# Splits and block sums around the change from the expert layer to the GLU: all on VectorE, begun in the seventh expert; the GLU's out-product between the two parts of a step

## The chip, the cores and the metric

The kernel runs on one core of a Trainium2 chip. The metric is the device time of one execution in microseconds, the median of several runs. Engines are named as in the profile: PE (TensorE matmul) with PEld (its weight loads), DVE (VectorE), ACT (ScalarE), POOL (GpSimd) and SP (SyncE, which issues most DMAs).

## What is computed

Three layers follow each other: a gated linear attention, a mixture of 8 experts of which each token takes one, and a bilinear GLU with an output matrix. The change touches the last expert steps and the GLU.

```python
# experts: N = 3072 tokens, D = 384, F = 1024
h = np.maximum(x[mask] @ w1[e], 0.0)
out[mask] = gate_w[mask, None] * (h @ w2[e])
# GLU: w1, w2 (384 x 1024), w3 (1024 x 1024), w_out (1024 x 384)
a = x @ w1
b = x @ w2
h = a * b @ w3
return (h @ w_out).astype(np.float32)
```

The kernel multiplies w3 by w_out beforehand (the tile wp), so the GLU is (a * b) @ wp.

## The kernel before

Every matrix product is made of three passes (PASSES): each fp32 operand is split into a high half (ACT rounds it to fp32r, L142) and a lower half (the rest, a subtraction on DVE or POOL, L143); the passes are high x high, high x lower and lower x high. `split` does both, and its last argument names the engine of the lower half, POOL (G) by default.

Experts (L1094 on). For each of 8 experts, 8 steps s run over 128 hidden columns: `g1_step` (9 matmuls into hb; ACT writes the high half of h, L994; DVE the lower, L995), then `g2_step` of the step before (9 matmuls into acc, which read h). A phase is half an expert: its two weight matrices come by DMA into two tiles `stg` (pool `stage`, two buffers), are split into wh and wl, and the splits stand in a queue of generators, `wsplit`, of which each step pulls a few. `bg` is a second such queue: it turns and multiplies w3 into wp (`w3_turn`, `w3_times` on PE, with pieces on ACT, DVE and POOL). Phases 16 and 17 are the two halves of the GLU's weights, kept in scratch `gd` (`prefetch_g`): `plain_sets` splits the first matrix, `mixed_sets` makes sums and differences of blocks of both (S1 to S4, A22, A23), since the GLU forms a and b from seven block products in place of more. `x_sets` does the same for a pair of token blocks: from six blocks of the expert output xd it makes nine split tiles, x0 to x8 (B11, T3, T2, T1, B21, B31, T4, B22, B32). Tile names end in h for the high and l for the lower half.

GLU (L1215 on). Tokens go in 3 pairs (n) of 2 x 512. The first part of a pair has 8 groups s. A group has 12 products (pa, pb, pc, pd), then 21 that add to them; ACT copies pa, pb and pd, DVE and POOL form the sums, and DVE multiplies. The product of the first block is split at once into a pair of tiles (abh and abl, in turn with two halves of a `stg` tile) and goes through `out_step` (12 matmuls of 384 columns with wp, L1199) behind the products of the next group; the product of the second block is kept in `later`. The second part of a pair splits the eight `later` blocks (`to_pair`) and runs 8 more out_steps (o2), while `x_sets(n + 1)` prepares the next pair; `store` copies the results and writes them by an indirect DMA from POOL's queue. m1t, m5t, m7t and ut are slices of two tiles xT. Of PSUM's two groups of four banks one takes a pair's products and then o2, the other o1; from pair to pair they change places.

Each engine runs its instructions in the order in which the code issues them; a tile that is written again waits for its readers.

## Time and profile before

| | us |
|---|---|
| median of 3 runs (736.49 to 738.60) | 738.53 |
| the profiled execution | 738.52 |
| its span (first to last instruction) | 736.5 |
| PE busy | 705.5 (96%) |
| DVE busy | 455.4 (62%) |
| ACT busy | 359.8 (49%) |
| POOL busy | 399.8 (54%) |

The page also cuts the span in 40 slices of 18.4 us; each digit is the busy share in tenths:

```profile
PE   8999999999999999999999787999999999999995
DVE  8989899976555555435424877455754448645551
ACT  5797878845657666546545542222422224322230
POOL 5366877784877677475456654222552223622243
PEclk9999999999999999999999998999999999999998
```

The experts run from about 177 to 429 us, the GLU from 429 to 728 us; the last 8 us hold the last stores.

### The profile page before, as it was taken

The numbers are of one execution on the slowest core, as the hardware profiler recorded it, in microseconds if no ns is written. First come the engines' busy times: TensorE is split into PE (matmuls) and PEld (weight loads), VectorE is DVE, ScalarE is ACT, GpSimd is POOL, SyncE is SP. The second block draws the span as 40 slices with busy tenths as digits, with TensorE's granted clock in tenths as the row PEclk, the third lists the DMA queues.
The fourth block names the chain that finished last, engine by engine and source line by source line (L and its number), as shares of the span: only waits on it lengthen the run. The fifth ranks groups of instructions, "written<-read, shape, count | busy, mean of one in ns | idle before, by whom it ended". The sixth has DMA issues, their size and how long they took to land.

```text
span 736.5 us, 13521 instructions
## 1 busy us (share of the span) xinstructions
PE 705.5 (96%) x5098; PEld 644.4 (87%) x5098; DVE 455.4 (62%) x828; ACT 359.8 (49%) x745; POOL 399.8 (54%) x464
## 2 busy tenths in 40 slices
PE   8999999999999999999999787999999999999995
PEld 7999988889999999999999665888888888888895
DVE  8989899976555555435424877455754448645551
ACT  5797878845657666546545542222422224322230
POOL 5366877784877677475456654222552223622243
PEclk9999999999999999999999998999999999999998
DMA  8999999653876776473442230000110001100001
GB/s 170 209 224 214 230 222 230 170 195 96 271 228 211 252 241 222 148 233 107 123 129 87 86 88 0 1 0 1 44 43 1 1 0 44 45 0 1 1 33 56
DMA packets 132032, 85.73 MB, mean 116 GB/s; under 512 B 106481, under 2 KB 114681, under 8 KB 131961
## 3 DMA queue, kind: packets, MB, share of 16 engines
q1 hardware_dynamic: 128489, 74.55, 37.3%
q0 software_dynamic: 3072, 9.46, 3.4%
q8 instruction: 42, 0.69, 0.4%
q10 hardware_dynamic: 400, 0.79, 0.3%
q14 instruction: 29, 0.24, 0.1%
HBM read 70.57 MB, written 14.22 MB: 115 GB/s over the span
## 4 chain that ended last, share of the span: by engine, by line
PE 58%; DVE 7%; DMA 3%; ACT 3%; issue 2%; POOL 2%; SPq 1%; POOLq 0%; DVEq 0%; ACTq 0%
PE acc L1006 11%; PE hb L992 10%; PE ob L1199 10%; PE pa L1161 7%; PE pb L1161 6%; PE pd L1161 6%; PE pc L1161 4%; DMA stg<-in_moe_w_dram 3%; PE wpb L185 3%; DVE wl L143 1%; PE xb L979 1%; ACT wh L142 1%; DVE stg L143 1%; DMA stg<-gd 1%; DVE h L1205 1%
## 5 line engine op out<-in xcount | busy, mean ns | idle before, releaser
L143 POOL TENSOR_TENSOR wl<-stg,wh 128x384 fp32r<-128x384 f32 (+1 forms) x110 | 128.5, 1197 | 56.4 <-ACT wh L142 54.6
L1164 POOL TENSOR_TENSOR xT<-xT,xT 128x512 f32<-128x512 f32 x48 | 62.8, 1308 | 132.9 <-ACT xT L1171 129.5
L1006 PE MATMUL acc<-h,wh 128*128 128x448 f32 (+7 forms) x384 | 105.5, 352 | 8.1 <-DVE h L995 7.9
L992 PE MATMUL hb<-xT,wh 128*128 128x448 f32 (+7 forms) x384 | 102.5, 348 | 0.0
L995 DVE SCALAR_TENSOR_TENSOR h<-hb,h 128x448 fp32r<-128x448 f32 (+7 forms) x64 | 37.0, 577 | 85.7 <-ACT h L994 85.4
L1006 PEld LDWEIGHTS acc<-h,wh 128*128 128x128 f32 x384 | 70.5, 188 | 12.8 <-DVE h L995 10.7
L142 ACT CAST wh<-stg 128x384 fp32r<-128x384 f32 (+1 forms) x121 | 61.1, 561 | 25.6 <-DMA stg<-in_moe_w_dram 21.0
L992 PEld LDWEIGHTS hb<-xT,wh 128*128 128x128 f32 x384 | 70.8, 188 | 1.4
L992 PE MATMUL hb<-xT,wl 128*128 128x448 f32 (+7 forms) x192 | 66.7, 348 | 0.0
L1006 PE MATMUL acc<-h,wl 128*128 128x448 f32 (+7 forms) x192 | 66.6, 347 | 0.0
L994 ACT ACTIVATE h<-hb 128x448 fp32r<-128x448 f32 (+7 forms) x64 | 32.3, 505 | 53.1 <-PE hb L992 52.9
L1164 DVE TENSOR_TENSOR xT<-xT,pc 128x512 f32<-128x512 f32 x48 | 32.8, 683 | 39.4 <-PE pc L1161 39.2
L1164 DVE TENSOR_TENSOR xT<-xT,pb 128x512 f32<-128x512 f32 x24 | 16.5, 689 | 64.3 <-PE pb L1161 64.2
L1199 PE MATMUL ob<-wp,abh 128*128 128x384 f32 x176 | 46.0, 343 | 0.0
L1199 PE MATMUL ob<-wp,stg 128*128 128x384 f32 x228 | 44.3, 338 | 1.1 <-DVE stg L143 1.1
L516 POOL TENSOR_SCALAR_AFFINE_SELECT am<-am 128x512 f32<-128x512 f32 x48 | 29.4, 637 | 25.7 <-ACT am L515 25.7
L1199 PEld LDWEIGHTS ob<-wp,stg 128*128 128x128 f32 x228 | 39.6, 188 | 3.8 <-DVE stg L143 3.0
L1170 ACT COPY xT<-pa 128x512 f32<-128x512 f32 x24 | 14.0, 585 | 56.2 <-PE pa L1161 53.8
L1206 POOL DMA_INDIRECT out_dram<-h,didx x24 | 24.2, 1010 | 27.0 <-DVE h L1205 24.6
L185 PE MATMUL wpb<-wo,w3t 128*128 128x384 f32 x192 | 36.8, 340 | 0.0
L1187 ACT CAST abh<-xT 128x512 fp32r<-128x512 f32 x13 | 8.1, 621 | 58.7 <-DVE xT L1164 40.6
L992 PEld LDWEIGHTS hb<-xT,wl 128*128 128x128 f32 x192 | 36.1, 188 | 0.7
(365 smaller groups left out, 1838.4 us busy)
## 6 DMA issues: line engine op xcount, KB each, us to landing
stg<-in_moe_w_dram SPq DMA_DIRECT2D x30, 768.0 KB
raw<-in_moe_w_dram SPq DMA_DIRECT2D x28, 512.0 KB
xs<-xsd SPq DMA_DIRECT2D x8, 675.5 KB
q<-in_q_dram SPq DMA_DIRECT2D x24, 192.0 KB
k<-in_k_dram SPq DMA_DIRECT2D x24, 192.0 KB
v<-in_v_dram SPq DMA_DIRECT2D x24, 192.0 KB
f<-in_f_logit_dram SPq DMA_DIRECT2D x23, 192.0 KB
raw<-in_moe_w_out_dram SPq DMA_DIRECT2D x8, 384.0 KB
```

The costliest lines, as they stand in the source:

```text
L142: A.copy(out=hi, in_=src)
L143: eng.tensor_tensor(out=lo, in0=src, in1=f32(hi), op=ALU.subtract)
L185: PE.matmul(out=o, lhsT=t[:, x, j, :], rhs=wo[:, y, j, :], start=(j + n == 0), stop=(j == KF - 1 and n == 2))
L516: G.affine_select(out=m[:, hb], in_=m[:, hb], pattern=[[0, NP], [1, P]], compare_op=ALU.is_ge, fill=0.0, base=0, channel_multiplier=-1)
L992: PE.matmul(out=b, lhsT=w[x][:, kk, cs], rhs=xT[e][y][:, kk, :], start=(kk + n == 0), stop=(kk == KD - 1 and n == 2))
L994: A.activation(out=h[0], in_=b, func=AF.Relu)
L995: V.scalar_tensor_tensor(out=h[1], in0=b, scalar=0.0, in1=f32(h[0]), op0=ALU.max, op1=ALU.subtract)
L1006: PE.matmul(out=acc[d], lhsT=w[x][:, s % 4, d * P:(d + 1) * P], rhs=hs[s][y], start=(s + n == 0), stop=(s == KF - 1 and n == 2))
L1161: PE.matmul(out=o, lhsT=w[a][i][:, cs], rhs=x[b][j], start=(first and m == 0), stop=(last and m == 2), skip_group_check=True)
L1164: eng.tensor_tensor(out=out, in0=a, in1=b, op=op)
L1199: PE.matmul(out=o[t], lhsT=ab[x][:, t * P:(t + 1) * P], rhs=wp[:, y, s, :], start=(s + m == 0), stop=(s == KF - 1 and m == 2), skip_group_ ...
L1206: ins = G.indirect_dma_start(out=out, out_offset=bass.IndirectOffsetOnAxis(ap=didx[:, j:j + 1], axis=0), in_=r, in_offset=None,)
```

## The change

- In `x_sets`, `plain_sets` and `mixed_sets` every lower half and every sum is DVE's; so are all lower halves of phases 13 to 15 (`ph > 2 * E - 4`; before, POOL's but for half of phase 15).
- `x_sets(0)` begins at step 3 of the seventh expert, with the pools of the GLU opened there, and a table X_AT spreads its 13 pieces over the seventh and eighth expert. Before, it took 3 pieces in each step of the eighth, some of them on POOL.
- `bg` is pulled 4 times per step in the sixth expert (before 3) and drained at step 3 of the seventh (before, step 0 of the eighth).
- The pulls of `wsplit` at the end change: in the eighth expert's steps 4 to 7 they are 3, 0, 3, 3 and 2 more at the end (before 4, 4, 4, 9), in the GLU's first groups 3, 3, 3, 9 (before 6, 9). The sums of `mixed_sets` come in another order and are made in the loaded tiles.
- In a GLU group, `out_step` of the group before stands between the 12 and the 21 products; the lower half of the product stands behind the last sum on DVE; one pair of tiles serves all first blocks.
- In the second part, the first out_step of o2 comes ahead of the last of o1, o1's results are copied by ACT, one per step, and POOL splits nothing.

```diff
-                split(t[:, i], h[:, i], l[:, i], V if ph in (0, 2 * E - 1) and i % 2 else G)
+                split(t[:, i], h[:, i], l[:, i], V if ph > 2 * E - 4 or ph == 0 and i % 2 else G)
...
     def plain_sets(hl, r):
         for kk in range(KD):
-            split(r[:, kk], hl[0][:, kk], hl[1][:, kk], V if kk % 2 else G)
+            split(r[:, kk], hl[0][:, kk], hl[1][:, kk], V)
             yield
...
+        if hf == 0:
+            s3(a, 2)
+            yield
+            one("A23", b, 2, (bh[:, 2], bl[:, 2]))
+            yield
+            s1()
+            s2()
+            yield
+            ch, cl = third[hf]()
+            one("S3", a, 2, (ch[:, 0], cl[:, 0]))
+            yield
+            one("S2", b, 0, (ch[:, 1], cl[:, 1]))
+            yield
+            one("S1", b, 2, (bh[:, 0], bl[:, 0]))
+            yield
+            one("A22", b, 1, (bh[:, 1], bl[:, 1]))
+            yield
+            s4(a, 1)
+            one("S4", a, 1, (ch[:, 2], cl[:, 2]))
+            yield
+            return
...
+        X_AT = (0, 0, 0, 1, 3, 0, 2, 0, 1, 0, 2, 2, 0, 3, 0, 0)
...
-            plus, e1, e2 = (V, G, V) if n else (G, V, V)
...
-                if e == E - 1:
-                    if s == 0:
-                        bg.drain()
-                        close_w3()
-                        cvx.close()
-                        open_m2()
-                        xs_ids(e)
-                        ahead_x = x_sets(0)
-                    step(ahead_x, 3)
+                if (e, s) == (E - 2, 3):
+                    bg.drain()
+                    close_w3()
+                    cvx.close()
+                    open_m2()
+                    ahead_x = x_sets(0)
+                if (e, s) == (E - 1, 2):
+                    xs_ids(e)
...
-                bg.pull(3)
-                wsplit.pull((4, 4, 4, 9)[s % 4] if e == E - 1 and s >= KF // 2 else (0 if e or s else 2, 3, 2, 2)[s % 4])
+                bg.pull(4 if e == E - 3 else 3)
+                wsplit.pull((3, 0, 3, 3)[s % 4] if e == E - 1 and s >= KF // 2 else (0 if e or s else 2, 3, 2, 2)[s % 4])
+                if e >= E - 2:
+                    step(ahead_x, X_AT[s + (e - E + 2) * KF])
...
+            if e == E - 1:
+                wsplit.pull(2)
             g2_step(e, KF - 1)
...
             tt(G, m7t, m7t, m5t)
+            then()
             product(ab, "A12", "B21", False, False)
...
-            then()
             tt(V, m1t, ut, bt)
             tt(V, m1t, m1t, ab, ALU.mult)
-            pair = next_pair()
-            A.copy(out=pair[0], in_=m1t)
+            A.copy(out=pairs[0][0], in_=m1t)
             tt(V, m5t, ut, at)
-            tt(V, pair[1], m1t, f32(pair[0]), ALU.subtract)
             tt(V, m7t, m7t, bb)
+            tt(V, pairs[0][1], m1t, f32(pairs[0][0]), ALU.subtract)
...
-                    wsplit.pull((6, 9, 0, 0, 0, 0, 0, 0)[s])
+                    wsplit.pull((3, 3, 3, 9, 0, 0, 0, 0)[s])
...
-            second = {0: to_pair(later[0], next_pair())}
-            out_step(o1, last, KF - 1)
+            out_step(o2, second[0], 0)
             if end:
                 for s in range(1, KF):
-                    second[s] = to_pair(later[s], free[s], G if s % 2 == 0 else V)
-                    if s == 2:
-                        store(o1, 2 * n * NT)
-                for s in range(KF // 2):
+                    second[s] = to_pair(later[s], free[s])
+                out_step(o1, pairs[0], KF - 1)
+                store(o1, 2 * n * NT, copy=A.copy)
+                for s in range(1, KF // 2):
                     out_step(o2, second[s], s)
...
             else:
                 ahead_x = x_sets(n + 1)
-                for s in range(KF):
+                second[1] = to_pair(later[1], pairs[1])
+                out_step(o1, pairs[0], KF - 1)
+                step(ahead_x, 1)
+                for s in range(1, KF):
                     if s + 1 < KF:
-                        second[s + 1] = to_pair(later[s + 1], next_pair())
+                        second[s + 1] = to_pair(later[s + 1], pairs[(s + 1) % 2 == 1])
                     out_step(o2, second[s], s)
-                    if s == 0:
-                        store(o1, 2 * n * NT)
+                    if s <= NT:
+                        store(o1, 2 * n * NT, (s - 1,), copy=A.copy)
                     step(ahead_x, 2)
```

How the instructions stand on two engines, before and after, at three places. A row is a line, an operation, its output, its inputs and its shape.

DVE in the middle of the eighth expert, before: h is the lower half that PE reads, x0l to x8l are `x_sets`, wl the weights' lower halves; the rest of them stand on POOL.

```order
L995 SCALAR_TENSOR_TENSOR h_5996<-hb,h_5995 128x376
L143 TENSOR_TENSOR x2l<-xd,x2h 128x512
L143 TENSOR_TENSOR x7l<-xd,x7h 128x512
L143 TENSOR_TENSOR x4l<-xd,x4h 128x512
L143 TENSOR_TENSOR wl<-stg,wh 128x384
L995 SCALAR_TENSOR_TENSOR h_6029<-hb,h_6028 128x376
L143 TENSOR_TENSOR x6l<-xd,x6h 128x512
L143 TENSOR_TENSOR x5l<-xd,x5h 128x512
L143 TENSOR_TENSOR wl<-stg,wh 128x384
L995 SCALAR_TENSOR_TENSOR h_6065<-hb,h_6064 128x376
```

The same engine and place, after:

```order
L1031 SCALAR_TENSOR_TENSOR h_5988<-hb,h_5987 128x376
L143 TENSOR_TENSOR wl<-stg,wh 128x384 x2
L143 TENSOR_TENSOR x7l<-xd,x7h 128x512
L143 TENSOR_TENSOR x4l<-xd,x4h 128x512
L1031 SCALAR_TENSOR_TENSOR h_6029<-hb,h_6028 128x376
L143 TENSOR_TENSOR wl<-stg,wh 128x384 x2
L1101 TENSOR_TENSOR xd<-xd 128x512
L143 TENSOR_TENSOR x6l<-xd,x6h 128x512
L1031 SCALAR_TENSOR_TENSOR h_6063<-hb,h_6062 128x376
L143 TENSOR_TENSOR wl<-stg,wh 128x512 x3
L1031 SCALAR_TENSOR_TENSOR h_6096<-hb,h_6095 128x376
```

Between two h stand up to four operations in both; all weights' halves and the subtraction (L1101, L1065 before) are now among them, and part of x_sets has gone to the seventh expert.

PE at the turn from one GLU group to the next, before: pc is the last product of a group, ob the out-product of that group's predecessor, pa the first product of the next.

```order
L1161 MATMUL pc<-x8h,wh 128x512
L1161 MATMUL pc<-x8l,wh 128x512
L1161 MATMUL pc<-x8h,wl 128x512
L1199 MATMUL ob<-wp,stg 128x384 x12
L1161 MATMUL pa<-x0h,wh 128x512
L1161 MATMUL pa<-x0l,wh 128x512
```

PE after, inside a group: pd ends the 12 products, pa<-x4h begins the 21.

```order
L1195 MATMUL pd<-x3h,wl 128x512
L1231 MATMUL ob<-wp,abh 128x384 x2
L1231 MATMUL ob<-wp,abl 128x384
L1231 MATMUL ob<-wp,abh 128x384 x2
L1231 MATMUL ob<-wp,abl 128x384
L1231 MATMUL ob<-wp,abh 128x384 x2
L1231 MATMUL ob<-wp,abl 128x384
L1231 MATMUL ob<-wp,abh 128x384 x2
L1231 MATMUL ob<-wp,abl 128x384
L1195 MATMUL pa<-x4h,wh 128x512
```

The 12 out matmuls have moved from the end of a group (of its predecessor's product) into the middle of the next.

DVE in one GLU group, before (xT_6214 holds m1t and m5t, xT_6215 holds m7t and ut):

```order
L1164 TENSOR_TENSOR xT_6215<-xT_6214,pc 128x512
L1164 TENSOR_TENSOR xT_6214<-xT_6215,pb 128x512
L1164 TENSOR_TENSOR xT_6214<-xT_6214,pa 128x512
L1164 TENSOR_TENSOR xT_6214<-xT_6215,pd 128x512
L1164 TENSOR_TENSOR abl<-xT_6214,abh 128x512
L1164 TENSOR_TENSOR xT_6215<-xT_6215,pc 128x512
L1164 TENSOR_TENSOR xd<-xT_6214,xT_6215 128x512
```

After:

```order
L1198 TENSOR_TENSOR xT_6215<-xT_6214,pc 128x512
L1198 TENSOR_TENSOR xT_6214<-xT_6215,pb 128x512
L1198 TENSOR_TENSOR xT_6214<-xT_6214,pa 128x512
L1198 TENSOR_TENSOR xT_6214<-xT_6215,pd 128x512
L1198 TENSOR_TENSOR xT_6215<-xT_6215,pc 128x512
L1198 TENSOR_TENSOR abl<-xT_6214,abh 128x512
L1198 TENSOR_TENSOR xd<-xT_6214,xT_6215 128x512
```

The lower half abl and the sum with pc have changed places.

## Rows read from the trace of the kernel before

**Rows 1.** Busy time by stage: stretch, its length, each engine's busy us, clock, DMA.

```profile
core 0: us, PE busy (x) PEld busy (x) DVE busy (x) ACT busy (x) POOL busy (x), PEclk, DMA share, GB/s
394.90:429.50 34.60, 26.87 (x146) 24.70 (x145) 26.86 (x32) 16.60 (x33) 18.75 (x14) 1.00 0.23 70
429.50:512.80 83.30, 77.83 (x338) 64.48 (x337) 46.37 (x65) 22.94 (x41) 28.95 (x21) 0.96 0.07 19
536.10:609.90 73.80, 73.80 (x337) 62.21 (x336) 36.35 (x56) 18.78 (x32) 24.39 (x24) 1.00 0.03 11
512.80:536.10 23.30, 22.24 (x122) 20.73 (x122) 18.11 (x29) 9.94 (x19) 11.21 (x13) 1.00 0.09 35
706.80:728.40 21.60, 21.55 (x122) 21.18 (x120) 9.12 (x17) 4.84 (x10) 11.86 (x18) 1.00 0.15 56
```

**Rows 2.** PE's waits from 395 us on: waiter, releaser, total us, times, longest.

```profile
PE acc L1006 <- DVE h L995: 7.7, 6, 2.1
PE pa L1161 <- ACT xT L1170: 3.2, 2, 2.8
PE pc L1161 <- DVE xT L1164: 2.2, 1, 2.2
```

**Rows 3.** Timeline of PE, eighth expert and first GLU pair: start, us, instruction, idle before.

```profile
399.11 0.51 PE L1006 MATMUL acc<-h,wh 128*128 128x376 f32 x2
...
399.63 0.51 PE L992 MATMUL hb<-xT,wh 128*128 128x376 f32 x2
...
447.29 0.78 PE L1161 MATMUL pc<-x8h,wh 128*128 128x512 f32 x1 [2.23 <-DVE xT L1164]
...
457.56 0.80 PE L1161 MATMUL pa<-x4h,wh 128*128 128x512 f32 x1 [2.82 <-ACT xT L1170]
```

**Rows 4.** The table by stretch, as rows 1, behind the two gaps.

```profile
448.00:452.00 4.00, 4.00 (x17) 3.76 (x16) 1.34 (x3) 0.23 (x1) 0.00 (x0) 0.66 0.00 0
456.00:460.00 4.00, 2.44 (x6) 1.98 (x7) 2.24 (x3) 2.08 (x4) 3.48 (x3) 0.70 0.00 0
```

**Rows 5.** Timelines of DVE, POOL and ACT in the eighth expert.

```profile
406.75 1.78 DVE L143 TENSOR_TENSOR x7l<-xd,x7h 128x512 fp32r<-128x512 f32 x1
...
410.33 0.53 DVE L995 SCALAR_TENSOR_TENSOR h<-hb,h 128x376 fp32r<-128x376 f32 x1
412.23 0.69 DVE L143 TENSOR_TENSOR x6l<-xd,x6h 128x512 fp32r<-128x512 f32 x1 [1.36 <-ACT x6h L142]
412.84 0.69 DVE L143 TENSOR_TENSOR x5l<-xd,x5h 128x512 fp32r<-128x512 f32 x1
...
404.53 4.86 POOL L143 TENSOR_TENSOR wl<-stg,wh 128x512 fp32r<-128x512 f32 x3
...
413.45 0.47 ACT L994 ACTIVATE h<-hb 128x376 fp32r<-128x376 f32 x1
```

**Rows 6.** Timelines of PE and POOL in one GLU group of the second pair.

```profile
592.60 0.39 PE L1161 MATMUL pa<-x0h,wh 128*128 128x512 f32 x1
...
595.39 0.39 PE L1161 MATMUL pa<-x4h,wh 128*128 128x512 f32 x1
...
600.22 2.25 PE L1199 MATMUL ob<-wp,stg 128*128 128x384 f32 x12
602.30 0.39 PE L1161 MATMUL pa<-x0h,wh 128*128 128x512 f32 x1
...
594.85 1.29 POOL L1164 TENSOR_TENSOR xT<-xT,xT 128x512 f32<-128x512 f32 x1 [6.97 <-ACT xT L1171]
```

**Rows 7.** The page's costliest groups: busy us, mean ns of one, idle before.

```profile
L1170 ACT COPY xT<-pa 128x512 f32<-128x512 f32 x24 | 14.0, 585 | 56.2 <-PE pa L1161 53.8
```

**Rows 8.** Timeline of DVE in the second part of the first pair.

```profile
532.80 1.37 DVE L143 TENSOR_TENSOR stg<-xT,stg 128x512 fp32r<-128x512 f32 x1 [0.35 <-ACT stg L142]
```

**Rows 9.** Timelines of PE and DVE in the sixth expert, transposes of w3 and their split.

```profile
346.46 1.04 PE L174 MATMUL w3b<-ident,g 128*128 128x128 f32 x8
347.26 0.60 PE L992 MATMUL hb<-xT,wh 128*128 128x388 f32 x2
...
347.72 1.29 DVE L177 TENSOR_TENSOR w3t<-w3b,w3t 128x512 fp32r<-128x512 f32 x2 [1.57 <-ACT w3t L176]
```

More of the change, by code (lines that the diff above doesn't have):

```diff
@@ L367, in mixed_sets, with one, s3, s1 @@
             d["A1%d" % (kk + 1)] = ah[:, kk], al[:, kk]
-        def one(n, t, kk, hl, eng):
+        def one(n, t, kk, hl):
             d[n] = hl
-            split(t[:, kk], hl[0], hl[1], eng)
-        one("A23", b, 2, (bh[:, 2], bl[:, 2]), V)
+            split(t[:, kk], hl[0], hl[1], V)
+        def s3(t, kk):
+            V.tensor_tensor(out=t[:, kk], in0=a[:, 0], in1=b[:, 0], op=ALU.subtract)
+        def s1():
+            V.tensor_tensor(out=b[:, 2], in0=b[:, 0], in1=b[:, 1], op=ALU.add)
@@ new lines, in s2, with s4 @@
+        def s2():
+            V.tensor_tensor(out=b[:, 0], in0=b[:, 2], in1=a[:, 0], op=ALU.subtract)
+        def s4(t, kk):
+            V.tensor_tensor(out=t[:, kk], in0=a[:, 1], in1=b[:, 0], op=ALU.subtract)
+        if hf == 0:
[19 more added lines that the diff above has]
+            return
@@ L374, in mixed_sets @@
+        one("A23", b, 2, (bh[:, 2], bl[:, 2]))
         yield
-        one("A22", b, 1, (bh[:, 1], bl[:, 1]), G)
+        one("A22", b, 1, (bh[:, 1], bl[:, 1]))
         yield
-        V.tensor_tensor(out=b[:, 2], in0=b[:, 0], in1=b[:, 1], op=ALU.add)
-        V.tensor_tensor(out=b[:, 1], in0=a[:, 0], in1=b[:, 0], op=ALU.subtract)
+        s1()
+        s3(b, 1)
         yield
-        V.tensor_tensor(out=b[:, 0], in0=b[:, 2], in1=a[:, 0], op=ALU.subtract)
+        s2()
+        one("S1", b, 2, (bh[:, 0], bl[:, 0]))
@@ L381, in mixed_sets @@
         yield
-        one("S1", b, 2, (bh[:, 0], bl[:, 0]), V)
+        s4(b, 2)
+        ch, cl = third[hf]()
+        one("S3", b, 1, (ch[:, 0], cl[:, 0]))
         yield
-        V.tensor_tensor(out=b[:, 2], in0=a[:, 1], in1=b[:, 0], op=ALU.subtract)
-        ch, cl = third[hf]()
+        one("S2", b, 0, (ch[:, 1], cl[:, 1]))
         yield
-        for i, (n, kk) in enumerate((("S3", 1), ("S2", 0), ("S4", 2))):
-            one(n, b, kk, (ch[:, i], cl[:, i]), V if i == 2 else G)
-            yield
+        one("S4", b, 2, (ch[:, 2], cl[:, 2]))
@@ L391, in prefetch @@
+        yield
     def prefetch(ph):
@@ L1193, in group @@
                 tt(V, t, m5t[:, c], m7t[:, c], ALU.mult)
-            return pair
         def out_step(o, ab, s, ts=range(NT)):
@@ L1199, in out_step, with store @@
                     PE.matmul(out=o[t], lhsT=ab[x][:, t * P:(t + 1) * P], rhs=wp[:, y, s, :], start=(s + m == 0), stop=(s == KF - 1 and m == 2), skip_group_check=True)
-        def store(o, j0, ts=range(NT)):
+        def store(o, j0, ts=range(NT), copy=V.tensor_copy):
             for t in ts:
@@ L1204, in store @@
                 r = f32(m1p.tile([P, CAP], F32R, name=f"h{j % 2}", bufs=3))[:, 0:DM]
-                V.tensor_copy(out=r, in_=o[t])
+                copy(out=r, in_=o[t])
                 ins = G.indirect_dma_start(
@@ L1217, in attn_moe_glu_kernel @@
             o1 = [bank2(1 - n % 2, DM, "ob") for _ in range(NT)]
-            last = None
             for s in range(KF):
-                pair = group(n, s, lambda: s and out_step(o1, last, s - 1))
+                if s == KF - 1:
+                    second = {0: to_pair(later[0], pairs[1])}
+                group(n, s, lambda: s and out_step(o1, pairs[0], s - 1))
                 if n == 0:
-                    wsplit.pull((6, 9, 0, 0, 0, 0, 0, 0)[s])
-                if n == 0 and s == 1:
+                    wsplit.pull((3, 3, 3, 9, 0, 0, 0, 0)[s])
+                if n == 0 and s == 3:
                     t = stage[0].tile([P, KD, 512], F32R, tag="stg", name="stg")
                     pairs.append([t[:, i] for i in range(2)])
-                last = pair
             o2 = [bank2(n % 2, DM, "ob") for _ in range(NT)]
-            free = list(xs_of.values())
-            second = {0: to_pair(later[0], next_pair())}
-            out_step(o1, last, KF - 1)
+            out_step(o2, second[0], 0)
             if end:
+                free = list(xs_of.values())
                 for s in range(1, KF):
-                    second[s] = to_pair(later[s], free[s], G if s % 2 == 0 else V)
-                    if s == 2:
-                        store(o1, 2 * n * NT)
-                for s in range(KF // 2):
+                    second[s] = to_pair(later[s], free[s])
+                out_step(o1, pairs[0], KF - 1)
+                store(o1, 2 * n * NT, copy=A.copy)
+                for s in range(1, KF // 2):
                     out_step(o2, second[s], s)
```

29 lines of the change are left out of this document (13 added, 16 removed).

## Prediction

> **What bounds the kernel now.** The page first: PE is busy 96% of the span, and its slices (the table above) fall below nine tenths only in the 23rd to 25th and at both ends. So time can come only from where PE stands still. The list of PE's waits [rows 2] names who lets it stand: in the eighth expert DVE's lower half of h (6 times, 7.7 us), in the first GLU pair ACT's and DVE's pieces of the sums (3.2 and 2.2 us). Next the table by stage [rows 1], which I read as pairs of stages with the same PE work.
> - Eighth expert, 34.6 us. Its PE work is 16 groups of 9 matmuls of 376 columns; three start 0.52 us apart [rows 3], at 399.11 and 399.63, so 48 x 0.52 = 25.0 us. Lost: 9.6 us.
> - First parts of the GLU pairs: 83.3 us for the first pair, 73.8 us for the second, same matmuls, and in the second PE is busy the whole time. Lost: 9.5 us. PE's idle time in it is 83.3 - 77.8 = 5.5 us; the other 4.0 are restarts and a slow clock: after the gaps of 2.23 and 2.82 us [rows 3] the granted clock is 0.66 and 0.70 of full speed over 4 us [rows 4], so part of them ran at the lower of the two levels, 1.2 in place of 2.4 GHz.
> - Second parts of pairs 1 and 2: 23.3 us (the row of the first stands; the second's is 23.3 too), against 21.6 us for the last pair, which has the same 120 out-product matmuls without a gap. The window of the last pair also holds the end of the group before it (some 0.2 us) and the tail of its last matmul (0.2 us), so 1.7 to 2.1 us are lost in each; I take 2.0.
>
> Together 9.6 + 9.5 + 4.0 = 23.1 us that PE stands, from three causes.
>
> Why DVE is late shows in [rows 5]. The lower half of a 512-column split takes 0.69 us on DVE, and the next one starts 0.61 us after it, when POOL rests (x6l, x5l). Beside POOL's three splits, which ran from 404.53 to 409.39, the same operation took 1.78 us (x7l). The x_sets subtractions on POOL (a sum is 1.29 us there [rows 6], against 0.69) also lie inside a chain ACT, DVE, POOL, ACT. So DVE was busy 26.9 of the eighth expert's 34.6 us [rows 1], and h waited behind it.
>
> **The change part by part.**
> *Eighth expert.* x_sets and the splits of phases 13 to 17 are DVE's alone, and x_sets(0) starts in the seventh expert (steps 3, 4, 6) in place of step 0 of the eighth. By the order, DVE's work of the eighth expert is now 27 lower halves or sums of at most 512 columns, 8 operations of h and 3 accumulator copies. POOL has nothing between its last split of phase 12 and the first GLU sum, so the price is the one without POOL: 27 x 0.61 = 16.5, 8 x 0.53 = 4.2, 3 x 0.6 = 1.8, in all 22.5 us of PE's 25.0. At the full 0.69 us each it is 24.6. It fits either way, and the end may run over, since the last six of the 27 are wanted only by the GLU. Where it is tightest, step 7: DVE has four operations behind h of step 6 (0.53 + 4 x 0.61 = 3.0 us) against a PE step of 3.12 us; then ACT's h (0.47 us [rows 5]), DVE's 0.53 and PE's 9 matmuls of the step before (1.56 us) leave some 0.3 us. I keep 0.3 us of the 9.6 as lost: gain 9.3. Bounds: 2.7 if DVE's own waits for ACT of the stage before (34.6 - 26.9 = 7.7 us) all stay, since then 22.5 + 7.7 = 30.2 us against 25.0 leave PE 5.2 late and a slow stretch costs 1.7 more (half of 4.0 less the restarts); 9.6 if it all goes.
>
> *Seventh expert.* It gets 20 lower halves and sums on DVE: 14 of phases 13 and 14, which were POOL's, and six of x_sets, which came in the eighth expert. At 0.61 us that is 12 us more on an engine that has 8 h, 3 x 0.55 us for xT, 3 copies and little else in a stage of some 31 us; the fullest step is some 2.9 us against a PE step of 3.2. Cost 0, cover: the slack of a whole PE step between a g1 and the g2 that reads its h. If that goes, a step's overrun appears in PE (rival 1).
>
> *Background, W3.* bg.pull(4) in the sixth expert and the drain at step 3 of the seventh move the w3 work ahead: PE's amount is the same. One piece is new: in step 3 of the sixth expert 8 transposes and 6 times-matmuls stand next to each other on PE, with a split between. [Rows 9] price it: transposes began at 346.46 and PE went on at 347.26; DVE's first lower half began at 347.72 and lasts 0.65, so the third matmul would start at 348.4 and not at 347.6. Cost 0.8 us; 0 if the half is early, 1.8 if both halves are awaited. The second such place (end of the sixth expert) splits the transposes in two halves, as before had elsewhere, cost 0. The load of phase 15's second matrix passes the write of the ids on SP, and the ids go two steps later: nobody waits for these but the last gather, cost 0.
>
> *First GLU pair.* The background of phase 17 is spread over groups 0 to 3 (3, 3, 3 steps and the rest) and no longer sits with 6 and 9 steps in groups 0 and 1, and POOL takes no split in it. Group 1, where PE stood 2.23 us before: DVE ends sum, abl and product of group 0 some 2.1 us into the step; three lower halves follow (1.8 us), then ut at 4.6 us. It is wanted by the last product, after 2.8 + 2.1 + 18 x 0.23 = 9.0 us. ACT, at 0.59 us each [rows 7]: three casts and the copies of pa and pb are done at 3.4 us, pa wanted at 4.9. Groups 2 and 3 come out with 1 us or more. Group 0 is the tight one: ACT's copy of pa stands behind the cast of S4, which waits for DVE's s4 (five sums after the last h); I get 0.25 us before PE wants it. I keep 0.3 of 9.5: gain 9.2, bounds 4.9 (one gap of 2.8 with its slow stretch, 1.7) and 9.5.
>
> *Out-product between the two parts of a step.* The step of a GLU group is [rows 6] 2.79 us for the first 12 products, 4.83 for the other 21, 2.08 for 12 out matmuls: the sum is the same in either order. The order on DVE puts abl behind the sum that waits for the last product pc. So abl is there 0.69 + 0.61 and some handing over, 1.4 us after the group's end; PE wants it at the third out matmul, 2.79 + 0.35 = 3.1 us after. Cost 0 with 1.7 us to spare. The copy of pa waits for abl (its tile is m1t): 2.0 us into the step, then pb 2.7, wanted at 4.9 and later: cost 0. POOL's two sums (1.29 us each) start then and end near 5.4, awaited at 9.7.
>
> *Second parts.* The first out-product of o2 comes ahead of o1's last and covers abl (2.1 us against 1.4). POOL's four splits go to DVE, o1's four copies to ACT, one per step. DVE then has three operations per step of 2.1 us (1.8 us) and no 1.37-us operations [rows 8]. Counted step by step at these prices, the last pair of halves comes 0.3 us late. I take 0.4 us lost of 2.0, gain 1.6 each, 3.2 in both; bounds 0 and 4.2. The last pair had no gap and has none: DVE has seven lower halves in 4.3 us while 4.2 us of out-products are ready. Its tail after PE is untouched.
>
> *Sum* on the profiled execution's 738.52 us (median 738.53): 738.5 - 9.3 - 9.2 - 3.2 + 0.8 = **717.6 us**, 2.8% faster. Best: 738.5 - 9.6 - 9.5 - 4.2 = 715.2.
>
> **Rivals.**
> 1. *DVE becomes the bound of experts seven and eight.* For it: 22.5 us of work in 25.0, one queue in which a sum waits for ACT and ACT waits for a sum. Against it: POOL's 1.78 us per operation go with POOL. Price: up to 6.6 us as above, and 1 us in the seventh: 719 to 725, say 721.5. The Trainium skill, Perfetto Trace Analysis, section Optimizing Scalar/DVE Operations, says that where DVE is saturated, giving work to Scalar or even GPSIMD may make sense; this change does the reverse, and by that sentence it would end here. The same paragraph adds that GPSIMD and DVE share an SBUF read port, so that offloading between them might not help; the 1.78 against 0.69 us of this trace sides with that.
> 2. *The first GLU group waits on ACT* behind the cast of S4: one gap like that of 2.82 us, with its slow clock, 717.6 + 4.3 = 722.
> 3. *Slower: the long operations on DVE are not POOL's doing* but come from ACT's or the DMAs' traffic. Then 27 operations of the eighth expert take some 1.6 us: 43 + 6 = 49 us against 34.6 now, and the seventh's 20 take 32 instead of 12, which with h and copies is 42 of 31 us. 738.5 + 14 + 10 - 12 = 750. It begins at (25.0 - 6.0) / 27 = 0.7 us per operation, where DVE fills PE's time, and eats the whole gain at about 1.3 us: (27 x 1.3 + 6 - 34.6) + (20 x 1.3 + 10 - 31) = 11.5 us. Against it: in the GLU, with ACT at work and POOL at rest, an operation stays at 0.69, as x6l's at 412.23 does beside ACT's casts.
> 4. *No gain:* the stalls come back elsewhere in the same size, 737.
>
> **How the numbers follow.** Forecast 0.70 (714 to 720), rival 1 0.15, rival 2 0.08, rival 3 0.04, rival 4 0.03. The range takes in the forecast with its bounds and most of rivals 1 and 2: 714 to 724. Outside stay rivals 3 and 4 (0.07), the ends of 1 and 2, and sums of several bounds. A measurement here tells some 0.3% (2 us) from no change; the forecast and rivals 1 and 2 are past it: faster 0.93, same 0.03, slower 0.04.
>
> **What would show it.** The eighth expert near 25.3 us, h no longer among PE's waits, DVE's lower halves at 0.69 us in experts seven and eight; the first parts of the first and second pair of equal length (73.8); second parts near 21.7; one new wait of PE for w3t in the sixth expert; abl never awaited in a GLU step. Wrong would be: lower halves above 1 us without POOL, a wait of PE for pa's copy or for S4, a clock row below 0.9 in the GLU.

## The result and the profile after

The changed kernel takes **714.88 us** (median of 6 runs, 712.64 to 718.84) against 737.58 us of the kernel before in the same comparison: ratio 0.970, 95% interval 0.967 to 0.973. The forecast was 717.6 us, range 714 to 724. The profiled execution of the changed kernel is the longest of the six, 718.84 us with a span of 717.1 us; in its second to fourth expert, which the change does not touch, it took 3.8 us more than the profile of the kernel before (table below).

Busy time by engine and the PE line of the slices, from the page of the changed kernel:

```profile
PE 698.7 (97%) x5098; PEld 641.6 (89%) x5098; DVE 454.4 (63%) x860; ACT 364.1 (51%) x757; POOL 345.1 (48%) x420
...
PE   7999999999999999999999999999999999999995
```

The dip in the 23rd to 25th slice is gone. PE's waits from 395 us on, the list that answers to [rows 2], has a head and no entry. The table by stage, with the columns of [rows 1]: eighth expert, first part of pairs 1 and 2, second part of pair 1, end of the last pair:

```profile
399.10:424.10 25.00, 25.00 (x146) 25.00 (x145) 19.53 (x36) 14.30 (x29) 0.00 (x0) 1.00 0.30 96
424.10:500.20 76.10, 76.10 (x350) 64.43 (x350) 50.39 (x75) 24.06 (x43) 22.56 (x16) 1.00 0.09 22
519.20:595.40 76.20, 76.20 (x350) 64.52 (x350) 36.32 (x58) 19.27 (x33) 24.93 (x24) 1.00 0.03 11
500.20:519.20 19.00, 19.00 (x109) 18.80 (x108) 15.76 (x27) 10.80 (x22) 4.36 (x8) 1.00 0.12 42
690.20:709.60 19.40, 19.39 (x110) 19.02 (x108) 8.23 (x15) 5.72 (x13) 9.12 (x14) 1.00 0.18 63
```

PE is busy through every stretch at full clock. A first part now holds seven out-products and a second part nine, where before it was six and ten ([rows 1]); so pairs are compared whole below. The eighth expert has no POOL operation at all, and DVE is busy 19.5 of 25.0 us.

The next table is worked out from PE's timeline of each kernel's profile: a stage runs from the start of its first product to the start of the next stage's. "6th + 7th" are two experts, "2nd to 4th" three whose code is the same in all kernels. The medians are of 2 to 10 runs each, taken beside the kernel before at 736.5 to 737.8 us. Since the three stages of the same code took 87.0 to 92.8 us from profile to profile, the experiments are read by their own stages.

| kernel | 2nd to 4th | 6th + 7th | 8th expert | pair 1 | pair 2 | last pair | median us |
|---|---|---|---|---|---|---|---|
| before | 87.8 | 62.8 | 34.57 | 106.5 | 97.1 | 95.2 | 737.6 |
| after | 91.6 | 63.8 | 24.96 | 95.1 | 95.1 | 95.3 | 714.9 |
| weight halves back on POOL | 92.8 | 64.0 | 24.96 | 95.1 | 95.1 | 95.3 | 717.4 |
| x_sets(0) late | 87.1 | 63.8 | 26.09 | 95.1 | 95.1 | 95.3 | 716.6 |
| out-product at the end | 88.2 | 63.7 | 24.96 | 96.5 | 95.1 | 95.2 | 714.7 |
| second part's halves on POOL | 87.0 | 63.8 | 24.96 | 97.1 | 97.1 | 95.3 | 718.5 |
| old engines, new order | 88.6 | 63.8 | 24.96 | 97.3 | 97.1 | 95.3 | 718.3 |
| new engines, old order | 90.6 | 62.8 | 30.20 | 103.3 | 96.1 | 95.2 | 729.6 |
| before, out-product in the middle | 89.4 | 62.8 | 34.47 | 100.8 | 97.9 | 96.9 | 733.9 |
| old engines, x_sets(0) late | 89.0 | 63.8 | 29.53 | 97.3 | 97.1 | 95.3 | 723.7 |
| old engines, sets in old order | 89.4 | 63.8 | 28.67 | 97.0 | 97.1 | 95.3 | 722.3 |
| POOL sums added | 89.1 | 63.8 | 30.90 | 95.1 | 95.1 | 95.3 | 721.4 |
| POOL fills added | 89.4 | 63.8 | 24.97 | 95.1 | 95.1 | 95.3 | 714.1 |
| three background steps | 92.1 | 62.8 | 24.96 | 95.1 | 95.1 | 95.3 | 713.7 |

From the first two rows, before rounding: 9.6 us come from the eighth expert, 11.4 from pair 1, 2.0 from pair 2; the sixth and seventh expert together cost 0.9 and the last pair 0.1. That is 22.0 us, and the medians differ by 22.7. The second to fourth expert took 3.8 us more in this profile; that is not the change, as the same code took 87.0 to 92.8 us in the fourteen kernels.

### The profile page after: what moved, and what is told of

Same layout as the page of the kernel before. It is cut to its first block, busy times and chain, and to the rows that moved or that the text cites. A ratio compares the mean times of both kernels' runs of the same rounds, so it can differ in the third digit from the quotient of the medians.

```text
span 717.1 us, 13516 instructions
## 1 busy us (share of the span) xinstructions
PE 698.7 (97%) x5098; PEld 641.6 (89%) x5098; DVE 454.4 (63%) x860; ACT 364.1 (51%) x757; POOL 345.1 (48%) x420
## 4 chain that ended last, share of the span: by engine, by line
PE 63%; DMA 5%; POOL 2%; issue 2%; ACT 2%; SPq 1%; DVE 1%; POOLq 0%; DVEq 0%; ACTq 0%
PE ob L1231 14%; PE acc L1042 10%; PE hb L1028 9%; PE pd L1195 7%; PE pb L1195 7%; PE pa L1195 7%; PE pc L1195 5%; DMA stg<-in_moe_w_dram 4%; PE wpb L185 3%; POOL wl L143 1%; DMA gd<-gt 1%; PE xb L1015 1%; ACT wh L142 1%; POOL gt L230 1%; PE w3b L174 0%
## 5 line engine op out<-in xcount | busy, mean ns | idle before, releaser
L143 POOL TENSOR_TENSOR wl<-stg,wh 128x384 fp32r<-128x384 f32 (+1 forms) x86 | 98.9, 1181 | 34.6 <-ACT wh L142 34.5
L1220 ACT CAST abh<-xT 128x512 fp32r<-128x512 f32 x24 | 14.9, 621 | 133.7 <-DVE xT L1198 133.7
L1231 PE MATMUL ob<-wp,abh 128*128 128x384 f32 x240 | 61.8, 338 | 0.0
L1231 PEld LDWEIGHTS ob<-wp,abh 128*128 128x128 f32 x240 | 44.0, 188 | 1.8
L1231 PE MATMUL ob<-wp,abl 128*128 128x384 f32 x120 | 40.5, 338 | 0.0
L1042 PEld LDWEIGHTS acc<-h,wl 128*128 128x128 f32 x192 | 36.1, 188 | 0.6
```

Source lines behind the costliest of these rows:

```text
L143: eng.tensor_tensor(out=lo, in0=src, in1=f32(hi), op=ALU.subtract)
L1042: PE.matmul(out=acc[d], lhsT=w[x][:, s % 4, d * P:(d + 1) * P], rhs=hs[s][y], start=(s + n == 0), stop=(s == KF - 1 and n == 2))
L1231: PE.matmul(out=o[t], lhsT=ab[x][:, t * P:(t + 1) * P], rhs=wp[:, y, s, :], start=(s + m == 0), stop=(s == KF - 1 and m == 2), skip_group_ ...
```

## Experiments: what the engines are worth, part by part

**Does the weight halves' engine matter?** The forecast named POOL's three splits of 4.86 us [rows 5] as the reason that DVE was late. Put back:

```
-                split(t[:, i], h[:, i], l[:, i], V if ph > 2 * E - 4 or ph == 0 and i % 2 else G)
+                split(t[:, i], h[:, i], l[:, i], V if ph in (0, 2 * E - 1) and i % 2 else G)
```

> The changed kernel, with one part undone: the lower halves of the expert weights of phases 13 and 14 are POOL's again, and those of phase 15 are dealt out between POOL and DVE as before; x_sets, the sums for the GLU and the order stay as changed. Theory P (beside a two-input POOL operation a DVE operation takes two to three times as long, and that is why h was late): POOL has 4 lower halves, some 6 us, in the eighth expert (24.96 us in the changed kernel); what DVE does meanwhile takes twice its time, some 4 us more, less 4 x 0.61 = 2.4 us that DVE no longer does: the eighth expert 26 to 29 us, PE waiting for h again, single lower halves on DVE over 1.2 us there. Theory C (what made h late was how much DVE work stood in one place, and the engine that splits is of no account): DVE has less to do than in the changed kernel, so 25.0 us and no wait for h.

The eighth expert stayed at 24.96 us, with no wait for h, as theory C had it. POOL's and DVE's timeline in it (start, us, instruction, idle before), as in [rows 5]:

```profile
403.13 1.30 POOL L143 TENSOR_TENSOR wl<-stg,wh 128x512 fp32r<-128x512 f32 x1 [4.47 <-ACT wh L142]
404.39 1.74 POOL L143 TENSOR_TENSOR wl<-stg,wh 128x512 fp32r<-128x512 f32 x1
...
403.66 1.32 DVE L143 TENSOR_TENSOR wl<-stg,wh 128x512 fp32r<-128x512 f32 x1 [0.53 <-ACT wh L142]
405.70 0.55 DVE L1031 SCALAR_TENSOR_TENSOR h<-hb,h 128x376 fp32r<-128x376 f32 x1 [0.72 <-ACT h L1030]
...
407.50 0.68 DVE L143 TENSOR_TENSOR x7l<-xd,x7h 128x512 fp32r<-128x512 f32 x1
```

The lengthening is there, 1.32 us beside POOL and 0.68 after it (and POOL's second half takes 1.74 in place of 1.30 us), and PE never notices: behind the long half DVE still stood idle 0.72 us until ACT had the high half of h ready. As far as a cost of the stage goes, theory P is wrong here, though its mechanism is seen.

**The same in the second parts.**

```
-                split(src, xs_of[name][0], xs_of[name][1], V)
+                split(src, xs_of[name][0], xs_of[name][1], G if n and name in ("B22", "B21", "B31", "B32") else V)
```

> The changed kernel, with the lower halves of B22, B21, B31 and B32 of the second and third pair on POOL again, in the second parts; o1's copies stay on ACT. Theory P: each of the two second parts loses 1 to 2 us (19.03 us for 9 out-products in the changed kernel, 23.3 for 10 before), with DVE operations of 1.2 us or more beside POOL's, 2 to 4 us in all. Theory C: POOL takes 2.4 us off DVE in each second part, PE waits for nothing as now, 0 us.

Pairs 1 and 2 lost 2.0 us each: theory P, with its price. POOL, DVE and PE late in the second part of pair 1, and behind them the same half in the changed kernel:

```profile
506.95 1.30 POOL L143 TENSOR_TENSOR x7l<-xd,x7h 128x512 fp32r<-128x512 f32 x1
508.20 1.28 POOL L143 TENSOR_TENSOR x4l<-xd,x4h 128x512 fp32r<-128x512 f32 x1
...
507.01 2.76 DVE L143 TENSOR_TENSOR abl<-xT,abh 128x256 fp32r<-128x256 f32 x1 [0.95 <-ACT abh L142]
...
509.83 0.45 PE L1231 MATMUL ob<-wp,abl 128*128 128x384 f32 x1 [1.02 <-DVE abl L143]
```

```profile
513.96 0.42 DVE L143 TENSOR_TENSOR abl<-xT,abh 128x256 fp32r<-128x256 f32 x1
```

A half of 256 columns, 0.42 us long in the changed kernel, took 2.76 us: it started just behind POOL's first operation and ended only after POOL's second. PE reads this half next and waited 1.02 us; in the eighth expert the delay of a weight half ran out before the next h. So the same contention costs 2.0 us here and nothing there. That it hangs on how soon PE reads what was delayed is argued from these rows; no run varies that alone.

**The contention by itself.** POOL gets work of its own in the eighth expert, on a tile that nobody else uses: two sums per step in one kernel, five fills (as long, but reading nothing) in the other.

```
sums:
+                    for _ in range(2):
+                        G.tensor_tensor(out=noise, in0=noise, in1=noise, op=ALU.add)
fills, the control:
+                    for _ in range(5):
+                        G.memset(noise, 0.0)
```

> The changed kernel with work added: in each of the 8 steps of the eighth expert POOL adds a 128x512 tile of its own, which nobody else reads or writes, to itself, twice. No dependency is added and no DVE operation. Theory P (POOL's two-input operations beside DVE's lengthen them): 16 x 1.3 us = 21 us of POOL in the 25 us; DVE's 27 lower halves and sums take 1.2 to 1.8 us in place of 0.69 while POOL works, DVE needs 27 x 1.3 + 6 = 41 us, and the stage grows from 24.96 to 33 to 41 us with PE waiting for h. Theory Q (what hurt in the kernel before was the chain from DVE to POOL and back, not the memory they share): nothing changes, DVE's operations stay at 0.69 us and the stage at 25 us.

> The control to the kernel with POOL's added sums: the changed kernel, with five fills of a 128x512 tile of POOL's own per step of the eighth expert in place of two sums: POOL as long at work (5 x 0.53 = 2.6 us per step), but it reads nothing and only writes. Theory P (DVE is slowed by POOL's two-input operations): DVE's operations stay at 0.69 us and the stage at 24.96 us. Theory W (any work of POOL on the shared memory slows DVE): DVE's operations over 1 us and the stage over 28 us.

The stage table, POOL and DVE of the kernel with sums, then of the one with fills:

```profile
394.80:425.70 30.90, 27.29 (x146) 26.40 (x145) 27.80 (x37) 14.16 (x29) 17.88 (x15) 0.94 0.25 77
...
396.24 1.04 POOL L1162 TENSOR_TENSOR xs<-xs 128x512 f32<-128x512 f32 x1
...
399.92 1.37 POOL L1162 TENSOR_TENSOR xs<-xs 128x512 f32<-128x512 f32 x1
...
401.37 1.37 POOL L1162 TENSOR_TENSOR xs<-xs 128x512 f32<-128x512 f32 x1
...
399.33 3.96 DVE L143 TENSOR_TENSOR wl<-stg,wh 128x512 fp32r<-128x512 f32 x3
...
403.21 0.54 DVE L1031 SCALAR_TENSOR_TENSOR h<-hb,h 128x376 fp32r<-128x376 f32 x1
```

```profile
395.40:420.40 25.00, 25.00 (x146) 25.00 (x146) 19.52 (x36) 14.30 (x29) 18.95 (x36) 1.00 0.30 96
...
399.81 1.90 DVE L143 TENSOR_TENSOR wl<-stg,wh 128x512 fp32r<-128x512 f32 x3
```

Three lower halves take 3.96 us beside sums (1.32 each) and 1.90 beside fills; the stage 30.90 and 24.97 us. So POOL's two-input work on other data, without any dependency, slows DVE's operations with two inputs in SBUF and costs 5.9 us here, part of it by a lower clock (last section). The expectation of 33 to 41 was too high: POOL's sums were through at 413.8 us, some 12 us before the stage's end. A fill costs nothing. The h operation, which reads PSUM and one SBUF tile, stays at 0.54.

POOL pays as well: its sum takes 1.04 us with no half beside it and 1.37 us beside one. The two then each do one operation in 1.45 us (399.92 to 401.37), little less than one behind the other, 1.04 + 0.61 = 1.65 us. The Trainium skill, SBUF — State Buffer, section SBUF: two separate sides, says just this of which operations conflict; it also says that the one that starts first blocks the other fully for the whole instruction. The trace agrees on the first. On the second it agrees where DVE's half waited through two POOL operations (2.76 us, above), and but for 0.2 us of overlap beside the sums.

## Experiments: the engines against the order

These two cross the change: the new order with the old engines, and the old order with the new engines.

```
new order with the old engines, against the changed kernel:
-                split(t[:, i], h[:, i], l[:, i], V if ph > 2 * E - 4 or ph == 0 and i % 2 else G)
+                split(t[:, i], h[:, i], l[:, i], V if ph in (0, 2 * E - 1) and i % 2 else G)
-            split(r[:, kk], hl[0][:, kk], hl[1][:, kk], V)
+            split(r[:, kk], hl[0][:, kk], hl[1][:, kk], V if kk % 2 else G)
-            split(t[:, kk], hl[0], hl[1], V)
+            split(t[:, kk], hl[0], hl[1], G if n in ('A22', 'S3', 'S2') else V)
-                V.tensor_tensor(out=out, in0=x, in1=y, op=ALU.subtract)
+                (V if n else G).tensor_tensor(out=out, in0=x, in1=y, op=ALU.subtract)
...
old order with the new engines, against the kernel before:
-            plus, e1, e2 = (V, G, V) if n else (G, V, V)
+            plus, e1, e2 = V, V, V
...
```

Left out in the first kernel are two edits that also go back to POOL: the four halves of the second parts, shown above, and every other half of o2 in the last pair. Left out in the second are the splits of the weights, of `plain_sets`, of `mixed_sets` and of o2, all turned to V (DVE).

> The changed kernel's order and places, with every lower half and sum of x_sets, of the weights and of the GLU's sets on the engine that had it before the change (x_sets(0)'s subtractions on POOL, the splits of phases 13 to 17 dealt out, four halves of later x_sets and three of o2's on POOL; only o1's copies stay on ACT). Theory E (the engine is what counts): the eighth expert near the 34.6 us of before, 31 to 35, the first GLU pair 3 us or more over its 76.2, each second part 2 us over 18.9. Theory O (the order is what counts): the eighth expert 25 to 26 us, first pair 76 to 77; only the second parts, whose loss from POOL another run has shown, 2 us each longer. Theory I (either of the two removes the loss in the eighth expert): like O there, and the kernel with the engines changed and the order of before is good there as well.

> The kernel before with the engines alone changed: every lower half and sum of x_sets, of phases 13 to 17 and of o2 on DVE, all places and the order as before (x_sets(0) in steps 0 to 4 of the eighth expert, phase 17 in groups 0 and 1, the out-product at the step's end, o1's copies on DVE). Theory E: eighth expert 25 to 28 us, and 3 us or more of the first pair's 9.5 come back. Theory O: the eighth expert stays at 31 to 35 us, with h waiting behind the crowd on DVE, the first pair at 83. Theory I: the eighth expert 25 to 28 us, since the engines alone are enough there.

The eighth expert and pair 1's first part of the new order with the old engines; then the eighth expert of the old order with the new engines, and its longest PE waits from 385 us on (columns as [rows 2]; the two left out, of out-products for DVE, are 1.4 us together):

```profile
394.20:419.20 25.00, 25.00 (x147) 25.00 (x146) 18.09 (x27) 14.27 (x29) 13.13 (x11) 1.00 0.31 96
419.20:495.40 76.20, 76.20 (x349) 64.26 (x348) 47.94 (x68) 23.73 (x43) 31.99 (x23) 1.00 0.09 22
```

```profile
396.40:426.60 30.20, 26.12 (x146) 24.71 (x145) 25.66 (x45) 16.51 (x33) 0.00 (x0) 1.00 0.30 95
...
PE acc L1006 <- DVE h L995: 4.1, 4, 2.0
PE pa L1161 <- ACT xT L1170: 3.2, 2, 2.8
PE pc L1161 <- DVE xT L1164: 1.6, 1, 1.6
```

Neither E nor I: with the new order the eighth expert takes 24.96 us on either set of engines, although POOL works 13.1 us of it; with the old order the engines bring 34.57 to 30.20, 4.4 of 9.6 us. In pair 1 the order alone brings 9.3 of 11.4 us (106.5 to 97.3, and 2.0 of the missing 2.2 are the second part's), the engines alone 3.3. The new order with the old engines came out as theory O has it, second parts included. The old order with the new engines lies between the theories: 30.20 us is under O's 31 to 35 and over E's 25 to 28. So in the eighth expert the order alone is enough, and the engines help in part as long as the order is old. What the old order does with DVE all to itself shows in the timelines of DVE, PE and ACT late in its eighth expert:

```profile
418.32 1.29 DVE L143 TENSOR_TENSOR wl<-stg,wh 128x512 fp32r<-128x512 f32 x2 [1.85 <-ACT wh L142]
419.53 0.68 DVE L377 TENSOR_TENSOR stg<-stg 128x512 f32<-128x512 f32 x1
...
420.97 0.69 DVE L380 TENSOR_TENSOR stg<-stg 128x512 f32<-128x512 f32 x1
421.58 0.54 DVE L995 SCALAR_TENSOR_TENSOR h<-hb,h 128x376 fp32r<-128x376 f32 x1
...
422.17 0.44 PE L1006 MATMUL acc<-h,wh 128*128 128x376 f32 x1 [2.02 <-DVE h L995]
...
417.66 1.14 ACT L142 CAST wh<-stg 128x512 fp32r<-128x512 f32 x2 [2.60 <-DMA stg<-gd]
```

Every operation has its short length, yet h is 2.0 us late: it stands behind two halves and three sums of phase 16, and the halves could start only when ACT had its data from a DMA.

**Which part of the order, in the eighth expert?** Both start from the new order with the old engines.

```
-        X_AT = (0, 0, 0, 1, 3, 0, 2, 0, 1, 0, 2, 2, 0, 3, 0, 0)
+        X_AT = (0, 0, 0, 0, 0, 0, 0, 0, 3, 3, 3, 3, 1, 0, 0, 0)
```

> The kernel with the changed order and the engines of before (its eighth expert took 24.96 us, as the changed kernel's), and x_sets(0) put back into steps 0 to 4 of the eighth expert, its subtractions on POOL as before. With all on DVE that move cost 1.1 us. Theory X (x_sets' place and POOL's part in it together made the loss of 9.6 us: a chain ACT, DVE, POOL, ACT beside POOL's splits): 3 to 6 us lost here, the eighth expert 28 to 31 us, the waits in its steps 1 to 4. Theory G (the order of the GLU's sets of phase 16 made the loss): 25 to 26 us, as with all on DVE.

```
-        if hf == 0:
...
-                wsplit.pull((3, 0, 3, 3)[s % 4] if e == E - 1 and s >= KF // 2 else ...)
+                wsplit.pull((4, 4, 4, 9)[s % 4] if e == E - 1 and s >= KF // 2 else ...)
```

The whole block goes with its first line; without it the sums of phase 16 come in the old order.

> The kernel with the changed order and the engines of before (eighth expert 24.96 us), and in it the order of before for the sets of phase 16 alone: its sums in the old order and places (S1 to S4 behind one another as the third phase, 4, 4, 4, 9 steps per step of the eighth expert in place of 3, 0, 3, 3); x_sets(0) stays begun in the seventh expert. Theory X (x_sets made the loss): 25 to 26 us. Theory G (sums of the sets stand on DVE ahead of h and wait for ACT's casts of data that a load has just brought; in the kernel before h of steps 5 to 7 was late 4.1 us behind them): 3 to 5 us lost, 28 to 30 us, with the waits in steps 5 to 7.

PE's waits for h from the eighth expert, of the first and of the second:

```profile
PE acc L1042 <- DVE h L1031: 2.9, 4, 1.1
...
PE acc L1042 <- ACT h L1030: 0.3, 1, 0.3
```

```profile
PE acc L1021 <- DVE h L1010: 1.9, 2, 1.3
...
PE acc L1021 <- ACT h L1009: 0.6, 1, 0.6
```

4.6 us for x_sets' place, 3.7 for the sets' order: 8.3 of the 9.6 us, so X and G each hold in part. The lists add up to 3.2 and 2.5 us; the rest of each loss is in PE's busy time, 26.29 and 26.05 us in place of 25.00. The waits behind x_sets came from 404 to 418 us, in steps 3 to 6 and not 1 to 4 as expected. No run has both parts put back, so whether they simply add up, and where the other 1.3 us come from, stays open. With all on DVE, x_sets' place is worth much less:

> The changed kernel, with only the place of x_sets(0) undone: its steps are taken 3, 3, 3, 3, 1 in steps 0 to 4 of the eighth expert, as before, still all on DVE. Theory P: DVE has 33 operations at 0.61 us and 6 us of h and copies, 26.1 us, and in steps 0 to 3 some 5 operations beside h in a PE step of 3.12 us: the eighth expert 26 to 29 us against 24.96, DVE's operations still at 0.69 us. Theory C: the crowding was the cause, so most of the loss of the kernel before is back, 31 to 35 us (34.57 before), with the seventh expert no longer.

It took 26.09 us, 1.1 more than the changed kernel, theory P's lower end, and theory C is out: 41 operations on DVE, 22.8 of 26.1 us busy, hardly made h late. What x_sets costs in the eighth expert thus hangs on both: late with the old engines 4.6 us, late with all on DVE 1.1, early with either 0. The old engines are also those of the weights' halves and of the sets; x_sets' own part on POOL was not tried alone.

## Experiments: the out-product's place

In the changed kernel, moved back behind the last product (`then()` moved, nothing else):

> The changed kernel, with only the out-product moved back behind the last product of a GLU step; the pair of tiles for ab is the one of the changed kernel. Theory M (the place matters by itself, since ACT's cast of ab has to wait until the out-product of the step before has read the tile, and the casts and copies queued behind it on ACT wait too): PE waits in the first pair, where ACT has the casts of phase 17 behind that cast, 1.5 to 5 us more in its first part (76.1 us now), and nothing in the second pair. Theory S (the gain of the first pair is from spreading phase 17 over four groups and from POOL's rest; the place is worth nothing, as the prediction priced it): both first parts within 0.5 us of the changed kernel's.

Pair 1 lost 1.4 us, pair 2 nothing: just under M's range, and above S's. The one entry of PE's waits from 395 us on:

```profile
PE pa L1195 <- ACT xT L1204: 0.8, 1, 0.8
```

In the kernel before, moved to the middle, nothing else:

> The kernel before with the out-product alone moved between the two parts of a GLU step; engines and places as before. By the prediction's pricing (the place is worth nothing, the first pair's loss is POOL's and phase 17's): first part of the first pair 83.5 us as before, within 1 us (it holds the same six out-products). By the reading that ACT's cast of ab waits for the out-product of the step before and holds up the casts and copies behind it (1.3 us was lost by moving it back in the changed kernel): 1.3 to 5 us less in the first pair, the second pair as before.

Pair 1 became 5.8 us shorter, more than the 1.3 to 5 expected, pair 2 0.8 and the last pair 1.7 us longer. By parts, from PE's timelines, pair 1's first took 79.03 us with seven out-products, 76.95 without the seventh (2.08 us [rows 6]), against 83.48 us before: 6.5 us less. ACT in group 1, first of the kernel before, then of this one (the number in brackets is the idle time before, with its releaser), and PE's wait behind it in this one:

```profile
451.77 0.62 ACT L1187 CAST abh<-xT 128x512 fp32r<-128x512 f32 x1 [10.27 <-PE ob L1199]
...
456.41 0.62 ACT L142 CAST xs<-stg 128x512 fp32r<-128x512 f32 x1 [0.71 <-DVE stg L384]
```

```profile
447.88 0.62 ACT L1187 CAST abh<-xT 128x512 fp32r<-128x512 f32 x1 [7.42 <-DVE xT L1164]
...
453.66 0.50 PE L1161 MATMUL pa<-x4h,wh 128*128 128x512 f32 x1 [0.71 <-ACT xT L1170]
```

Before, the cast of ab waited for PE's out-product of the step before, at the very end of the step, and the casts of phase 17 and the copy of pa, which PE wants, stood behind it on ACT: 2.82 us [rows 3]. With the out-product in the middle the cast waits for DVE only and PE waits 0.71 us. The kernel with the new engines and the old order still has that wait, 2.8 us in its list above, with no POOL split beside it: it is the place's, not POOL's. The longer second and last pair go with the half done change: there o1's last product follows the group at once, with o2's first not yet ahead of it, and PE waits for abl, up to 0.7 us at a time.

## Experiment: the sixth expert

```
-                bg.pull(4 if e == E - 3 else 3)
+                bg.pull(3)
```

> The changed kernel with three steps of the background per step in the sixth expert as elsewhere, in place of four: w3's last transposes and products come later, the rest of them in one piece at step 3 of the seventh expert. Forecast's theory (the four steps put transposes and products next to each other, and PE waits 0.8 us for the half between them; 1.4 us is what the sixth expert grew): the sixth expert back at 31.5 us (32.9 in the changed kernel), and the piece in the seventh costs less than that, total 0 to 1.4 us shorter. Rival (the lump in the seventh expert holds PE's queue while the add of POOL, ACT's copy and DVE's half follow one another): the seventh expert 1 to 3 us longer than 30.85, nothing won.

The sixth expert of the changed kernel, PE's and POOL's timeline:

```profile
347.84 0.66 PE L174 MATMUL w3b<-ident,g 128*128 128x128 f32 x4 [0.72 <-POOL g L230]
348.25 0.95 PE L185 MATMUL wpb<-wo,w3t 128*128 128x384 f32 x4
...
342.07 4.46 POOL L143 TENSOR_TENSOR wl<-stg,wh 128x512 fp32r<-128x512 f32 x3
346.50 1.28 POOL L230 TENSOR_TENSOR g<-raw,g 128x512 int32<-128x512 int32 x1
```

The one wait of PE there, 0.72 us, is for POOL's add of the w3 piece, which stood behind three weight halves, and not for DVE's half between transposes and products: those start 0.4 us after the transposes. With three steps throughout, sixth and seventh expert take 31.51 + 31.27 us against 32.91 + 30.84, 1.0 us less; the rest of w3 in the seventh costs 0.4 us, and no wait of PE is left from 330 us on. The median, 713.69 us (ratio 0.966, 0.963 to 0.969), is the shortest here, though by medians alone it is not told from the changed kernel.

## Why the prediction was right, and where it was not

- **Eighth expert, 9.3 us; measured 9.6.** The 25.0 us of PE's work [rows 3] were the right floor, and DVE's work fitted into it as summed (22.5 us forecast, 19.5 busy in the stage); the 0.3 us kept back for step 7 were not lost. What failed is the cause in "Why DVE is late": POOL's neighbourhood, with the engines as the remedy. The row (1.78 against 0.69 us [rows 5]) was read rightly for DVE, and the added sums show that it can cost 5.9 us; that POOL's splits beside it were long too, 4.86 / 3 = 1.62 us each, was not read. But with the order new, POOL at work 13.1 us costs nothing, and with the order old, DVE alone still loses 5.2 us. The forecast treated the moved steps as a matter of fitting DVE's total into 25.0 us; what counts is what stands ahead of each h, and whether that waits for ACT, POOL or a DMA. That the size came out is partly luck: the change held the moved steps too, and the forecast saw in them only a lighter sum for DVE.
- **First GLU pair, 9.2 us; measured 9.3** (11.4 for the whole pair less 2.1 for its second part). Size right. The step that failed is "Cost 0" of the out-product: it looked at PE's sum, at abl and at DVE, and not at the tile of ab that the out-product holds and at ACT's queue behind the cast that waits for it. By itself the move is worth 6.5 us in the old kernel and 1.4 in the new one. That the spread of phase 17 leaves less behind the cast there is the likely reason, but no run undid the spread alone, so its share of the 9.3 us is not shown. The engines' part, in the first part of the pair, is 0.2 us with the new order (76.44 against 76.23 us with POOL back, from PE's timeline). Rival 2's wait did not come. The bound given as 4.9 is 5.0 by its own terms (9.5 - 2.8 - 1.7).
- **Second parts, 1.6 us each; measured 2.1.** The term was mis-sized by the 0.4 us thought late at the end: PE is busy 19.00 of 19.00 us. Here the engines are the cause as forecast: 2.0 us when four halves return to POOL.
- **New wait in the sixth expert, 0.8 us; measured 0.7 as a wait and 0.9 in the two stages,** with the wrong releaser: POOL's add, not DVE's half. [Rows 9] were read for DVE only; POOL's queue in the changed order was not followed.
- **Tail and abl, 0;** right: the last pair is 0.1 us longer, and abl is in no wait of the changed kernel.
- **Rivals.** Rival 1, with the Trainium skill's sentence from Perfetto Trace Analysis, Optimizing Scalar/DVE Operations, fell: DVE was busy 19.5 of 25.0 us. Its advice to hand work to GPSIMD, given for a DVE that is saturated, has its measure here: nothing gained or lost in the eighth expert in the new order, 2.0 us lost in each second part. Rival 3 is answered by sums against fills: the long operations are POOL's doing.
- The sum was right for a mixed reason: each stage's loss was read off a stage without it, and that held whatever removed the loss. What causes the loss of the eighth expert was only argued, and that was the part that fell.

## What to carry over

A stage's loss is best sized by the same stage without gaps, but that says nothing on which edit brings it back; an edit that only moves a step can be worth as much as what waits behind it in an in-order queue, so follow every tile that the moved step reads to the engine that wants to write it next. What moving work from POOL to DVE pays depends on what PE waits for: 2.0 us in each second part, where PE reads the delayed half next, 4.4 us in the eighth expert in the old order, nothing there in the new one. Before h, or any operation that PE waits for, nothing should stand that itself waits for a load or for a third engine.
